# Values of the sink tokens by eight small transfers instead of selection matmuls, with a new order table

## The chip, the cores and the metric

The kernel runs on one core of one Trainium2 chip. A time is the device time in microseconds (us) of one execution. Before the change it is 243.45 us, the median of three runs (242.84, 243.45 and 244.1).

A core has five engines that each work through a list of instructions in order: PE (TensorE, matmuls; its weight loads are shown apart as PEld), DVE (VectorE), ACT (ScalarE), POOL (GpSimd) and SP (SyncE, which here only issues transfers). Matmuls write to PSUM, which has eight banks; everything else lies in SBUF. Transfers (DMAs) are issued by POOL, where an instruction of 0.7 to 1 us builds the descriptors, or by SP and ACT, and all of them are carried by the same 16 DMA engines.

## The reference

Two steps, in float32 at the reference and mostly bfloat16 in the kernel. First attention with a window of 128 keys and four "sink" keys (the first four of each sequence), for 4 batches, 8 heads, 768 positions and 64 values a head:

```python
scores = scale * np.matmul(q, k.transpose(0, 1, 3, 2))
keep = is_sink | in_window            # pos < 4, or 0 <= rel < 128
scores = np.where(keep, scores, -1e9)
a = np.exp(scores - max); a = a / (sum(a) + 1e-9)
x = np.matmul(a, v)                   # then (B*S, H*D) = (3072, 512)
```

Then a gated feed-forward layer on the 3072 rows:

```python
xn = x / np.sqrt(np.mean(x * x) + 1e-6) * rms_g
g = xn @ w_gate;  val = xn @ w_val    # 512 -> 1536
out = (g * sigmoid(g) * val) @ w_out  # 1536 -> 512
```

## The kernel before

**Tiling.** The 3072 rows are 24 blocks of 128 (g = 0 to 23; batch b = g // 6, place t = g % 6), and six groups G of four blocks for the feed-forward part. For each block the q, k and v tiles are loaded (POOL casts them to bfloat16 on the way; the first q and k come as float32 on SP's queue and are cast by DVE or ACT). q and k are turned to have the head's values on partitions: the first eight blocks by PE transposes with a copy (line 492, operations kp and qp), the others by a DMA transpose that SP issues (line 506). Then come scores (PE, lines 532, 548, 610), exp (ACT), masks (DVE, or POOL for late blocks), the product with v (av, lines 649 to 671), the division by the row sums (DVE; each v tile has a 65th column of ones that gives the sums), the root mean square and the scaling (xr, line 714), and the transposition of x (PE for the first eight blocks, line 729; a DMA transpose on SP from block 8 on, line 741). The feed-forward part follows: gate (g) and value (v) products, line 1000, tanh on ACT, two multiplications on DVE (lines 1013, 1023), the output product (o, line 1033), its copy to SBUF by ACT (line 1041) and a store of 256 KB issued by SP (line 1045).

**The sinks.** For the blocks with t of 2 and more the four sink keys lie outside the window. Their scores for all eight heads are made in one small product (ss, line 772), so that partition 32 x + 4 i + s (x = h // 2, i = h % 2) of the tile esk holds the exponential for head h and sink s. To multiply it with the values in one matmul (line 653), the tile vsk must hold, on partition 32 x + 4 i + s, the value row of sink s in the columns of head h and zero in the columns of the other heads. It is made in two halves for each batch: a matmul with the constant sel (line 754) copies the first four rows of v to all partitions, and DVE multiplies the result from PSUM with the head mask headm (line 763), two matmuls and two multiplications per batch, eight of each in all.

**The order.** The program is written as a list of some 1058 operations, numbered as they are declared. Each has a cost, what it needs and what it gives. The order on each engine is a table written out by hand (ORDER, lines 146 to 205), one list of numbers an engine. The class Plan (lines 35 to 143) goes through the table with its costs and its model of the transfers (land, line 59), to merge the five lists into one order of emission and to give each PSUM product a bank. Waits between engines follow from the data: an engine does not pass an instruction whose operands are not there, even where later ones could run. The parts that matter here:

- POOL's list begins with two selects for the constants ident and bias (lines 338, 344), then the loads: q and k of block 1, v of block 0, blocks 2 and 3 and the gate and value weights interleaved, then q of block 4, v of block 3, and so on. Only so many POOL loads are outstanding at a time; the next issue waits for a landing.
- PE's list begins with small matmuls on a zero tile (warm, line 468) among the first real work.
- SP's list has k and q of block 0 and the row of the scaling weights, then nothing until the DMA transposes of block 8 (near 47 us in the profile), with x transposes and stores from then on.
- DVE's list begins with the memsets.

## Time and profile before

| | before |
|---|---|
| median of three runs | 243.45 us |
| the profiled execution | 242.75 us |
| its span, first to last instruction | 241.0 us |
| PE busy | 235.0 us (98%) |
| DVE busy | 187.0 us (78%) |
| ACT busy | 122.3 us |
| POOL busy | 89.9 us |
| read from and written to HBM | 28.31 and 6.29 MB |
| matmuls of line 754 (vs) | 8, of 128 x 260 |
| multiplications of line 763 (vsk) | 8, 0.42 us each |

The profile is one execution. Its page lists the busy time of each engine, then the span in 40 slices (a digit is a busy share in tenths; PEclk is the TensorE clock that was granted, as a share of full speed), the DMA queues, and the chain of work that ended last. Other views cut out a stretch of time, list the instructions of an engine in order, or collect the instructions that touch one tile. Matmuls are pipelined: the duration of one in the profile includes its drain, which overlaps the next one, so the start of the next tells what it took of PE's time. A load's landing is the moment its semaphore is complete. A number in the text that isn't in a quoted line is a start, an end or a landing from the same trace.

### The profile page before, as it was taken

What the parts mean: (1) busy time and instruction counts of PE and PEld (TensorE: products, weight loads), DVE (VectorE), ACT (ScalarE), POOL (GpSimd) and SP (SyncE); (2) the same over time, 40 slices, a digit from 0 to 9 for tenths busy, and PEclk for the clock granted to TensorE, in tenths of its full rate; (3) what the DMA queues carried; (4) which work ended last, traced back from release to release, by engine and by line L of the source; (5) the groups of instructions that cost most, each with busy time, mean ns of one, the idle gap of its engine ahead of it and who ended that gap; (6) DMA issues with size and microseconds to landing.
All of it is one profiled execution on the core that took longest, in us unless ns stands there. A gap on an engine that the chain in (4) does not pass through costs nothing.

```text
span 241.0 us, 5846 instructions
## 1 busy us (share of the span) xinstructions
PE 235.0 (98%) x2324; PEld 149.8 (62%) x2324; DVE 187.0 (78%) x482; ACT 122.3 (51%) x267; POOL 89.9 (37%) x116
## 2 busy tenths in 40 slices
PE   6999999999999999999999999999999999999994
PEld 3469987875788676786886544445545444444443
DVE  2489979998999999999998999974599965436430
ACT  3775577477867565346754373461762222304211
POOL 8976885587555475200062123045340000000000
PEclk9679999999999999999999999999999999999999
DMA  9999999999999999999997809510241130103014
GB/s 125 148 183 188 184 184 187 164 136 150 141 137 149 180 165 146 159 180 169 141 153 70 109 0 112 115 40 0 87 47 22 21 112 0 69 18 131 3 50 167
DMA packets 113581, 27.38 MB, mean 114 GB/s; under 512 B 103697, under 2 KB 110609, under 8 KB 113554
## 3 DMA queue, kind: packets, MB, share of 16 engines
q0 software_dynamic: 81760, 13.90, 77.5%
q1 hardware_dynamic: 31650, 12.99, 29.8%
q8 instruction: 18, 0.29, 0.5%
q10 hardware_dynamic: 144, 0.13, 0.2%
q14 instruction: 9, 0.07, 0.1%
HBM read 28.31 MB, written 6.29 MB: 144 GB/s over the span
## 4 chain that ended last, share of the span: by engine, by line
PE 85%; DMA 7%; POOL 5%; issue 0%; DVE 0%; POOLq 0%
PE o L1033 25%; PE v L1000 24%; PE g L1000 23%; DMA wv<-in_moe_w_val_dram 4%; DMA q<-in_q_dram 3%; PE s L610 3%; PE av L668 2%; PE av L663 2%; PE av L653 2%; POOL wg L446 1%; POOL q L400 1%; POOL v L404 1%; PE o_last L1051 1%; POOL k L400 1%; PE s L532 1%; POOL wv L446 1%
## 5 line engine op out<-in xcount | busy, mean ns | idle before, releaser
L1000 PE MATMUL v<-xnt,wv 128*128 128x128 bf16 (+2 forms) x528 | 73.3, 282 | 0.0
L1000 PE MATMUL g<-xnt,wg 128*128 128x128 bf16 (+2 forms) x528 | 70.9, 282 | 0.0
L1033 PE MATMUL o<-wo,hT 128*128 128x512 bf16 x276 | 67.7, 379 | 0.0
L1007 ACT ACTIVATE th<-g 128x512 bf16<-128x512 f32 x72 | 41.6, 600 | 45.0 <-PE g L1000 40.0
L1013 DVE SCALAR_TENSOR_TENSOR p<-th,g 128x512 bf16<-128x512 bf16 x72 | 47.5, 682 | 17.6 <-ACT th L1007 17.4
L1000 PEld LDWEIGHTS <-wg 128*128 128x128 bf16 x528 | 43.2, 98 | 19.6 <-DMA wg<-in_moe_w_gate_dram 0.2
L1023 DVE TENSOR_TENSOR hT<-p,v 128x512 bf16<-128x512 bf16 x72 | 47.8, 682 | 9.6 <-PE v L1000 8.9
L1000 PEld LDWEIGHTS <-wv 128*128 128x128 bf16 x528 | 42.7, 98 | 19.9 <-issue 0.7
L1033 PEld LDWEIGHTS <-hT 128*128 128x128 bf16 x276 | 25.7, 98 | 26.0 <-issue 0.4
L644 POOL TENSOR_SCALAR_AFFINE_SELECT e<-e 128x512 bf16<-128x512 bf16 x20 | 12.6, 652 | 51.1 <-ACT e L619 50.8
L619 ACT ACTIVATE e<-s 128x384 bf16<-128x384 f32 x52 | 22.8, 498 | 15.4 <-PE s L610 15.3
L404 POOL DMA_DIRECT2D v<-in_v_dram x24 | 21.4, 890 | 9.1 <-DMA q<-in_q_dram 5.7
L690 ACT ACTIVATE sq<-x 128x512 bf16<-128x512 bf16 x24 | 15.3, 636 | 17.9 <-DVE x L682 17.7
L400 POOL DMA_DIRECT2D k<-in_k_dram x23 | 20.4, 888 | 8.5 <-DMA wo<-in_moe_w_out_dram 2.7
L400 POOL DMA_DIRECT2D q<-in_q_dram x23 | 20.5, 890 | 7.7 <-DMA k<-in_k_dram 4.5
L1041 ACT ACTIVATE osb<-o 128x512 f32<-128x512 f32 x23 | 13.5, 602 | 19.0 <-PE o L1033 19.0
L682 DVE TENSOR_TENSOR x<-av,rden 128x256 bf16<-128x256 f32 x48 | 20.4, 425 | 1.7
L714 DVE SCALAR_TENSOR_TENSOR xr<-x,r,gb 128x512 bf16<-128x512 bf16 x24 | 18.0, 752 | 0.8
L668 PE MATMUL av<-v,e 128*128 128x65 bf16 x192 | 17.8, 196 | 0.2
L583 ACT ACTIVATE e<-s 128x512 bf16<-128x512 f32 (+1 forms) x36 | 16.0, 528 | 2.8 <-PE s L532 2.3
L663 PE MATMUL av<-v,e 128*128 128x65 bf16 x160 | 15.5, 193 | 0.0
L668 PEld LDWEIGHTS <-e 128*128 128x128 bf16 x192 | 13.4, 99 | 2.6 <-DVE e L594 0.4
(78 smaller groups left out, 199.8 us busy)
## 6 DMA issues: line engine op xcount, KB each, us to landing
out_dram<-osb SPq DMA_DIRECT2D x23, 256.0 KB, 2.3
v<-in_v_dram POOLq DMA_DIRECT2D x24, 128.0 KB, 9.7
q<-in_q_dram POOLq DMA_DIRECT2D x23, 128.0 KB, 10.0
k<-in_k_dram POOLq DMA_DIRECT2D x23, 128.0 KB, 9.5
wo<-in_moe_w_out_dram POOLq DMA_DIRECT2D x2, 768.0 KB, 11.0
wg<-in_moe_w_gate_dram POOLq DMA_DIRECT2D x5, 256.0 KB, 8.2
wv<-in_moe_w_val_dram POOLq DMA_DIRECT2D x5, 256.0 KB, 8.6
stage<-in_k_dram SPq DMA_DIRECT2D x1, 256.0 KB, 3.2
```

Source lines behind the costliest of these rows:

```text
L400: nc.gpsimd.dma_start(out=T[name, g], in_=block_of(src, g))
L404: nc.gpsimd.dma_start(out=V16[b][:, t, :, 0:D], in_=block_of(v, g))
L619: nc.scalar.activation(out=e_tile(g)[:, x:x + 2, 0:TW], in_=BANK.pop(("s", g, u, hi))[:, 0:2 * TW].rearrange("p (j c) -> p j c", c=TW), fu ...
L663: nc.tensor.matmul(out=dest, lhsT=T["e", g - 1][:, x, P:2 * P], rhs=V16[b][:, t - 1, h, :], start=(t == 1), stop=False, skip_group_check=True,
L668: nc.tensor.matmul(out=dest, lhsT=T["e", g][:, x, 0:P], rhs=V16[b][:, t, h, :], start=(t == 0), stop=True, skip_group_check=True,)
L682: nc.vector.tensor_tensor(out=T["x16", g][:, 4 * u:4 * u + 4, :], in0=pvv[:, :, 0:D], in1=rden.unsqueeze(2).to_broadcast((P, 4, D)), op=AL ...
L714: nc.vector.scalar_tensor_tensor(out=T["xr", g], in0=T.pop(("x16", g)).rearrange("p h d -> p (h d)"), scalar=r[:, 3:4], in1=gb, op0=ALU.mu ...
L1000: nc.tensor.matmul(out=ps[:, i * n:(i + 1) * n], lhsT=w_sb[:, kt, ft * P:(ft + 1) * P], rhs=T["xnt", G][:, kt, cols], start=(kt == 0), sto ...
L1007: nc.scalar.activation(out=T["th", key], in_=BANK[("g", key)], func=ACT.Tanh, scale=0.5,)
L1013: nc.vector.scalar_tensor_tensor(out=T["p1", key], in0=T.pop(("th", key)), scalar=1.0, in1=BANK.pop(("g", key)), op0=ALU.add, op1=ALU.mult,)
L1023: nc.vector.tensor_tensor(out=T[hk][:, i:i + n, cols], in0=T.pop(("p1", key)).rearrange("p (n c) -> p n c", n=n), in1=BANK.pop(("v", key)) ...
L1033: nc.tensor.matmul(out=BANK[("o", G, tb)], lhsT=T["h", G, ft // 4][:, ft % 4, tb * P:(tb + 1) * P], rhs=wo[:, ft, :], start=(ft == 0), sto ...
```

## The change

The matmuls with sel, the tile sel and the copy that made it go. A tile vsink (128 x 4 batches x 65, float32) is set to ones by a DVE memset; eight transfers on SP's queue, one a head, put the four sink rows of v of all batches on partitions 32 x + 4 i to 32 x + 4 i + 3 (each 4 partitions x 4 batches x 64 values). For each batch one DVE multiplication of 128 x 520 makes vsk from vsink and headm. The 65th column stays one, as in the v tiles.

The planner's transfer model is changed: POOL loads are counted less late (a factor of 1.15 for 1.4 early on; 450 ns instead of 1000 ns added after 9 us), SP's transposes and stores 300 ns later. All five lists of the table are new. Since the numbers shift by nine behind the constants, the lists are told here by name:

- POOL: the first load (q of block 1) comes ahead of the two selects, bias then ident; k,2 and q,2 change places, as do some of the weight loads: the last four gate blocks now come in the order 10-11, 8, 9, ahead of all of value 8 to 11, whose order is 9, 10-11, 8. q of block 4 follows the same loads as before.
- DVE: the memset of vsink is first, then bias, ident, zeros; the constant masks come before the casts, and both first casts (k and q of block 0) are DVE's. The product vsk of batch 0 stands behind the scaling of block 0 by its sums and ahead of its xr; that of batch 1 stands among the multiplications of group 0.
- SP: after the row of scaling weights the eight small transfers (heads 6, 1, 4, 5, 3, 2, 7, 0). The DMA transposes begin q8, q9, k8, q10, k9, q11, k10, k11, then the store of block 3, q12, k12, the store of block 0, q13, q14, k14, the store of block 1, k13, k15, x8, q15, x9. Before, it was q8, k8, q9, k9, q10, q11, k10, k12, k11, q13, q12, the store of block 1, k13, q14, the store of block 0, q16, x8, x9.
- PE: k of block 1 is turned before the first scores. The list from the first gate product up to the turning of q of block 4 has the same members. Later, units move by up to some us; the scores of blocks 11 and 12 and the gate products of group 2 come earlier among the rest.

The core of the diff, and SP's list:

```diff
-            r["POOL"] = begin + (1.4 * work if begin < 8500 else work)
+            r["POOL"] = begin + (1.15 * work if begin < 8500 else work)
...
-            return r["POOL"] + 520 + (1000 if r["POOL"] > 9000 else 0)
+            return r["POOL"] + 520 + (450 if r["POOL"] > 9000 else 0)
...
-        return r["TR"] + (550 if ring == "TR" else 850) + min(late, 5000)
+        return r["TR"] + (850 if ring == "TR" else 1150) + min(late, 5000)
...
     "SP": """
-14 16 18 312 313 327 328 342 357 343 372 358 393 371 646 394 408 641 438 326 341 423 651
+23 25 27 21 16 19 20 18 17 22 15 315 330 316 345 331 360 346 361 653 374 375 638 393 408
...
-    sel = const.tile([P, P], BF16, name="sel")
+    vsink = const.tile([P, B, VW], FP32, name="vsink")
...
-    def make_sel():
-        nc.vector.tensor_copy(
-            out=sel.rearrange("p (a s) -> p a s", s=NS),
-            in_=ident[:, 0:NS].unsqueeze(1).to_broadcast((P, P // NS, NS)),
-        )
+    def make_headm():
...
+    dve(260, lambda: nc.vector.memset(vsink, 1.0), gives=["vsink1"], prio=-95)
+
+    def load_sink(h):
+        r = h // 2 * SW + h % 2 * NS
+        nc.sync.dma_start(
+            out=vsink[r:r + NS, :, 0:D], in_=v[:, h, 0:NS, :].rearrange("b s d -> s b d"),
+        )
+
+    for h in range(H):
+        sp(430, 2600, lambda h=h: load_sink(h), ["vsink1", "grow"], [("vsink", h)], -70 + h)
...
-    def sink_v(b, half):
-        nc.tensor.matmul(
-            out=bank(("vs", b, half))[:, 0:HW], lhsT=sel,
-            rhs=V16[b][:, 0, 4 * half:4 * half + 4, :], start=True, stop=True,
-        )
...
+    def sink_v(b):
+        T["vsk", b] = sink.tile([P, H, VW], BF16, name="vsk")
         nc.vector.tensor_tensor(
-            out=T["vsk", b][:, hs, :],
-            in0=BANK.pop(("vs", b, half))[:, 0:HW].rearrange("p (h c) -> p h c", c=VW),
-            in1=headm[:, hs].unsqueeze(2).to_broadcast((P, 4, VW)), op=ALU.mult,
+            out=T["vsk", b], in0=vsink[:, b:b + 1, :].to_broadcast((P, H, VW)),
+            in1=headm.unsqueeze(2).to_broadcast((P, H, VW)), op=ALU.mult,
         )
```

## The prediction

> **What bounds the kernel now.** I read the page first, for the busiest engine and the granted clock, then the windows by stage.
>
> ```profile
> span 241.0 us, 5846 instructions
> ...
> PE 235.0 (98%) x2324; PEld 149.8 (62%) x2324; DVE 187.0 (78%) x482; ACT 122.3 (51%) x267; POOL 89.9 (37%) x116
> ...
> PEclk9679999999999999999999999999999999999999
> DMA  9999999999999999999997809510241130103014
> ```
>
> ```profile
> 6.00:12.00 6.00, 5.80 (x46) 2.97 (x44) 2.99 (x15) 4.71 (x13) 6.00 (x9) 0.68 2.06 148
> 12.00:18.00 6.00, 5.76 (x78) 3.99 (x76) 4.82 (x20) 4.50 (x14) 4.51 (x6) 0.75 1.55 183
> ...
> 24.00:30.00 6.00, 6.00 (x108) 5.84 (x106) 5.50 (x10) 3.27 (x7) 5.14 (x6) 1.00 1.70 185
> ...
> 100.00:120.00 20.00, 20.00 (x241) 15.31 (x239) 18.73 (x51) 12.14 (x27) 0.00 (x0) 1.00 1.50 159
> ```
>
> The second fence gives a stretch, its length, the busy time of PE, PEld, DVE, ACT and POOL, the granted clock, the DMA share and GB/s. From 24 us on PE is never idle at full clock. A busy PE can still be slow, so I compared start-to-start times with widths: after 21 us the sum of all lost time is under 1 us. So behind 21 us PE's own work is the time; only less PE work, or a new wait, changes it.
>
> Next the chain of waits up to 32 us, and PE in order of time around its last line:
>
> ```profile
> 14.14 9.69 DMA wv<-in_moe_w_val_dram
> 23.84 0.30 issue
> 24.13 7.73 DMA q<-in_q_dram
> 31.86 0.05 issue
> 31.91 0.23 PE q L492
> ```
>
> ```profile
> 26.94 3.90 PE L1000 MATMUL g<-xnt,wg 128*128 128x128 bf16 x64
> 30.68 1.13 PE L1000 MATMUL v<-xnt,wv 128*128 128x128 bf16 x16
> 31.91 0.40 PE L492 MATMUL q<-ident,q 128*128 128x128 bf16 x4
> ```
>
> The transposition of q of block 4 waits for a load that lands at 31.86, 0.26 us after PE is ready; that load could be issued only when an older one had landed. So whatever PE gains before 32 us it hands back there: this landing starts the long saturated stretch. PE's work list ahead of that transposition has the same members in both tables (but for the two selection matmuls of batch 0), so the new table can't fill the wait.
>
> **The matmuls that go.** The rows of the tile vs, and one of its matmuls in order of time with its follower:
>
> ```profile
> L754 PE MATMUL vs<-v,sel x8: 274/274/398, 9.0 to 136.8; 128*128 128x260 bf16 x8
> L763 DVE TENSOR_TENSOR vsk<-vs,headm x8: 419/421/429, 9.5 to 138.1; 128x260 bf16<-128x260 f32 x8
> ```
>
> ```profile
> 57.62 0.27 PE L754 MATMUL vs<-v,sel 128*128 128x260 bf16 x1
> 57.73 0.81 PE L1033 MATMUL o<-wo,hT 128*128 128x512 bf16 x3
> ```
>
> The 274 ns include the overlapped drain; the slot is 57.73 - 57.62 = 0.11 us. Two of the eight lie before 14 us, where their 0.2 and 0.3 us vanish in the wait for q; six lie in the saturated stretch: five of 0.111 and one of 0.122, **-0.68 us**, all on the path.
>
> **DVE.** Per batch two multiplications of 0.42 us become one of 520 columns. The nearest row below is 128x512 at 0.68 (line 1023), the end above 0.84; I take 0.69, so 0.6 us less in all. The copy into sel (0.27) goes; the memset of vsink is added, from the memsets of 64 and 128 words (0.11, 0.17) about 0.30. DVE is 94% busy from 40 to 140 us, but PE doesn't wait for it; its cover is the PE stream. Nothing for the end. The product of batch 1 moves to about 28.6 us, where DVE has 0.23, 0.55 and 0.32 us idle before 33.5, enough for its 0.69. The memset stands first on DVE and delays the memsets of bias, ident and zeros by up to 0.5 us: the warm-up matmuls start at about 1.6 instead of 1.06, in time for the k block that lands at 4.05.
>
> **SP, start.** Eight issues at 0.45 to 0.57 us (the three issues now there) keep SP until about 6.2 us; its next instruction now comes at 47 us, so nothing queues behind them. They move 8 x 4 KB = 32 KB. Their price is in the DMA, which is full. The nearest transfers are the stage loads:
>
> ```profile
> stage<-in_k_dram SPq DMA_DIRECT2D x1, 256.0 KB, 3.2
> stage<-in_q_dram SPq DMA_DIRECT2D x1, 256.0 KB, 3.9
> ```
>
> Issued at 0.81 and 1.32, they land 1.2 us apart, so 256 KB cost 1.2 us and 32 KB cost 0.15, if spread like those. At worst they all lie on a quarter of the engines and hold each later load 0.6. The Trainium skill (DMA: Bandwidth & Descriptors, "Why a DMA increments its semaphore by 16 and not by 1") speaks for the worst: the engine count follows the slowest dimension, so a four-partition transfer uses four engines, the lowest-numbered. By that rule the sum would be 0.45 us higher than by the row; the trace names no engine, so it does not decide.
>
> **POOL, start.** The first load is issued ahead of the two selects: at about 0.8 (when SP starts) instead of 1.76, the later ones 0.35 earlier (0.8 + 1.01 + 0.29 + 0.25 + hops, against 2.77). But from 8 us on the loads wait on transfers, not issue (issue to landing grows from 4.5 to 9.7 us). Gain 0 to 0.35, and the first load now competes with the q stage load: its cast may be 0.5 to 0.9 late, repaid by the shorter PE list up to 18 us. Landing of q,4: -0.2 to +0.6; I take **-0.1** (0.25 gained, 0.15 paid, after the row of the same kind).
>
> **The new order behind 32 us.** I laid PE's new list out from q,4, each unit with its start-to-start time of before, and set it against landings. SP's list is what matters, since it waits in order:
>
> ```profile
> 71.44 2.64 SPq L506 DMA_TRANSPOSE qkT<-q  x2
> 74.18 0.57 SPq L1045 DMA_DIRECT2D out_dram<-osb  x1
> ```
>
> ```profile
> DMA to landing us min/median/max: 2.4/7.9/9.3
> ```
>
> The first is SP in order of time, where its first store goes out; the second is of the q and k transposes (line 506). The new list issues two stores and one more transpose before 71 us. The scores of block 12 move from 84.2 to 80.6; they need a transpose that was issued at 71.44 and landed at 80.13: 0.5 us to spare instead of 3. The first gate matmul of group 2 moves from 98.35 to 96.8 and needs the transpose of x of block 9. SP gives it out after k,15 has landed (82.89) and three transposes of 1.24: 86.6, plus 7.9 is 94.5. Three more transfers of 0.9 to 1.2 us ahead push it to 97.2 to 98.1. So the new wait is 0 (its 2.3 us to spare hold) to 1.3; with the longest latency, 9.3, it is 2.7. Latencies now don't grow with more transposes under way (8.1 us for one issued with one other under way, 8.1 with five), so I stay near the low end: **+0.4**. Lateness of several places doesn't add up, because each pushes all behind it.
>
> Sum: -0.68 - 0.1 + 0.4 = -0.38 on a span of 241.0. The profiled execution took 242.75 us in all, 0.70 below the median of 243.45 (242.84 to 244.1); I put the change on the median: **243.1 us**. About 0.5%, 1.2 us, is what this kernel's measurement can tell from no change.
>
> **Rivals.**
> 1. *Late transposes (the other side).* The moved stores hold the loads and SP's list back, and PE stands before block 12 or group 2. For: DMA at 9 tenths until slice 21, PE 98% busy, so no cover. Against: PE hardly waits today with the same latencies. Price 2.0 to 2.7, net +1.2 to +1.9: 244.7 to 245.4. It decides from 2.0 us of waiting on (0.78 gained, 1.2 to the bound). Chance 0.28.
> 2. *Small transfers on four engines.* q,4 at +0.45 beside my value: 243.5. Chance 0.14.
> 3. *A wait in place of the matmul.* The product of batch 0 stands on DVE ahead of the first block's scaling and waits for all eight transfers. The last issue is at about 5.7; with 3.9 us, as the stage load, it lands at 9.6, before the 10.9 at which DVE comes to it. With 7.9, as the transposes, 13.6: scaling 2 us late, then 2.3 us to spare on PE, no loss. Only past 14.5 does it cost: 0.5 to 1: 243.8. Chance 0.05.
> 4. *No new wait, loads 0.35 early.* -0.68 - 0.2: 242.6, and 242.3 if the 0.26 us at q,4 and the 0.15 us that PE waits at 28.7 go too. Chance 0.18.
> 5. *The clock.* It is 0.68 and 0.75 in 6:18, granted half from 8.2 to 15.0. One more half-rate stretch as long as half of that (3.4 us) costs up to 1.7, less 0.7 us of idle PE up to 32: +1.0, 244.1. The Trainium skill (TensorE: Matmul & The Clock Gate, "What's actually happening") says that the gate judges activity in free-running windows of about 3.4 us, so moving PE's work by half a microsecond may lose or win a whole window; the trace agrees in length, 6.8 us being two. Chance 0.05.
>
> The forecast has 0.30. The bound of faster is 242.2, and the runs of before spread by 0.6 us to each side: half of rival 4 and a fifth of the forecast fall below it, 0.15. Slower (244.7) is rival 1 and 0.05 of rivals 2, 3 and 5, 0.33; the rest, 0.52, is within 0.5%. Range: from the low draws of rival 4 (242.2) into rival 1 (245.2). The likeliest alone: 242.6 to 243.6.
>
> **What would show it.** No vs row, eight more SP issues near 2.4 to 6.2 us; the wait at q,4 still there within 0.5 us of 31.86; PE busy 20.00 in each 20 us behind it. Wrong if PE shows idle time before block 12's or group 2's matmuls over 1 us, if q,4 lands past 32.5, or if the end is 1.2 us earlier, which nothing here pays for.

## The result, and the profile after

The changed kernel takes 244.85 us (median; 244.42 to 245.46), against 243.45 (242.83 to 244.1) for the kernel before beside it: a ratio of 1.0056, 95% interval 1.0039 to 1.0073. It is slower by 1.4 us, where 0.35 us less was forecast.

The page of the changed kernel: its span, the busy time by engine, then the granted clock and the DMA share in 40 slices.

```profile
span 242.7 us, 5866 instructions
...
PE 232.4 (96%) x2316; PEld 148.9 (61%) x2316; DVE 187.8 (77%) x481; ACT 119.9 (49%) x264; POOL 90.0 (37%) x116
...
PEclk9999999999999999999999999999999999999999
DMA  9999999999999999999630999321300332001204
```

Less PE work and a longer span: 2.6 us less busy, 1.7 us more span. The clock was full from 8.4 us on in this execution, where the profiled one of before had it at half from 8.2 to 15.0. (The row PEclk has no record of the first microseconds and shows them as full. PE's matmuls of 128 columns start 0.107 us apart up to 8.4 us and 0.056 us behind that, so PE ran at half rate there; in the kernel before it did so up to 4.7 us, and again from 8.2 to 15.0.) That is where part of the 2.6 us comes from, and it bought nothing: the first gate matmul starts 0.97 us earlier (16.87 for 17.84), and the turn of q of block 4 (q,4 from here on; a turn is the transposition of a q or k block) starts at 32.13 for 31.91.

The windows of the changed kernel, columns as in the prediction (stretch, length, busy time of PE, PEld, DVE, ACT, POOL, clock, DMA share, GB/s):

```profile
12.00:18.00 6.00, 4.30 (x79) 3.40 (x77) 4.67 (x21) 5.04 (x16) 4.63 (x7) 1.00 1.65 180
...
24.00:30.00 6.00, 5.82 (x105) 5.64 (x103) 5.13 (x11) 2.77 (x5) 4.95 (x7) 1.00 1.66 186
...
36.00:44.00 8.00, 7.33 (x118) 5.12 (x116) 6.96 (x19) 4.92 (x12) 4.36 (x5) 1.00 1.70 187
80.00:86.00 6.00, 5.50 (x67) 4.16 (x65) 5.59 (x22) 1.91 (x6) 4.52 (x7) 1.00 2.11 155
...
100.00:120.00 20.00, 20.00 (x242) 15.09 (x240) 18.74 (x51) 11.44 (x28) 0.87 (x1) 1.00 1.48 156
135.00:142.00 7.00, 6.41 (x54) 3.43 (x51) 6.22 (x22) 3.23 (x8) 4.37 (x5) 1.00 1.65 148
```

PE is full between 100 and 120 as before, and has holes in 36:44, 80:86 and 135:142. The view of PE's waits from 22 to 145 us names them (line, what it waited for, us in total, times, longest); for the kernel before the same view has no line at all:

```profile
PE k L498 <- DMA k<-in_k_dram: 0.7, 1, 0.7
PE g L993 <- DMA xnt<-xr: 0.6, 1, 0.6
PE s L538 <- DMA qkT<-q: 0.5, 1, 0.5
PE g L993 <- DMA wg<-in_moe_w_gate_dram: 0.4, 1, 0.4
PE v L993 <- DMA wv<-in_moe_w_val_dram: 0.2, 1, 0.2
```

And where they stand, PE in order of time (start, length, what, idle time before it):

```profile
32.13 0.40 PE L498 MATMUL q<-ident,q 128*128 128x128 bf16 x4
...
41.14 0.40 PE L498 MATMUL k<-ident,k 128*128 128x128 bf16 x4 [0.67 <-DMA k<-in_k_dram]
...
82.35 0.61 PE L538 MATMUL s<-qkT 64*128 64x256 bf16 x8 [0.51 <-DMA qkT<-q]
...
139.52 1.69 PE L993 MATMUL g<-xnt,wg 128*128 128x512 bf16 x7 [0.59 <-DMA xnt<-xr]
```

Three waits behind the turn of q,4: the turn of k of block 5, the scores of block 12, the first gate of group 3. From here on a wait is counted from start to start: the time from the start of the matmul before, less what that matmul takes of PE when nothing is late. That gives 0.834, 0.669 and 0.755 us, more than the idle times shown, which leave out the drain of the matmul before. (The idle time at k of block 5 is put down to its load, which landed at 41.09.) The sum is 2.26 us.

**The balance closes.** From the start of q,4's turn to the start of the last output matmuls (o_last) the trace gives 234.93 - 31.91 = 203.02 us before and 236.58 - 32.13 = 204.45 after. Take the waits away: 203.02 - 0.12 = 202.90 before (0.12 in all, near 43 us), 204.45 - 2.26 = 202.19 after. The difference, 0.71, is the 0.68 of the six matmuls. So the matmuls' time was gained, and waits that weren't there before took it and 1.4 us more.

**Why these transfers are late.** SP's queue in order of time, the changed kernel from 63 us:

```profile
63.38 3.23 SPq L512 DMA_TRANSPOSE qkT<-k  x2
66.71 0.54 SPq L1038 DMA_DIRECT2D out_dram<-osb  x1
67.43 1.25 SPq L512 DMA_TRANSPOSE qkT<-q  x1
68.77 1.28 SPq L512 DMA_TRANSPOSE qkT<-k  x1
70.11 0.57 SPq L1038 DMA_DIRECT2D out_dram<-osb  x1
74.55 6.83 SPq L512 DMA_TRANSPOSE qkT<-q  x2
```

SP had its two stores out at 66.7 and 70.1 and stood free at 70.7. It waited for the load of q of block 13, whose turn went out at 74.55, where before it went out at 71.44. That load was issued at 59.74 (59.46 before) and landed at 74.53 (71.42 before); k of block 13, issued at 60.60, at 77.03 (72.38). The queues of both kernels between 60 and 72 us, from the issue of this load on (packets, MB, time of the packets as a share of 16 engines' span), before:

```profile
q0 software_dynamic: 8423, 1.06, 144.9%
q1 hardware_dynamic: 2370, 0.57, 51.7%
```

and after:

```profile
q0 software_dynamic: 6406, 0.81, 112.5%
q1 hardware_dynamic: 3547, 0.86, 73.8%
```

q0 carries POOL's loads, q1 what SP issues; in this stretch that is turns alone, since the data of the two stores moves behind 72 us. The sum is nearly the same (1.63 and 1.67 MB), but the turns have 0.29 MB more and the loads 0.25 MB less. The new list sends its turns up to those of block 12 closer together, and what they move arrives while q and k of block 13 wait for theirs. (Between 70 and 78 us, the stretch that an expectation below speaks of, SP's queue moved 0.92 MB for 0.41. There the excess is the data of the two stores, 256 packets of 2 KB, and the turns' part is as before, 0.40 for 0.41 MB.) Sharing need not be all of it. Between the issue and the landing of q of block 13 the DMA engines stood nearly idle, at 3 tenths or under in slices of 0.2 us, for 1.8 us in three gaps (1.0 us in two gaps before); no run here shows what makes these gaps.

The gate of group 3 is another place: on SP the x of block 14, which was ready at 121.39, stands behind the x of block 15, which DVE finished at 133.06. It went out at 134.32 and PE waited for it until 139.52.

**The start.** POOL in order of time:

```profile
1.32 1.01 POOL L406 DMA_DIRECT2D q<-in_q_dram  x1 [0.80 <-POOLq L1137]
2.42 0.30 POOL L344 TENSOR_SCALAR_AFFINE_SELECT bias<-bias 128x128 bf16<-128x128 bf16 x1
2.67 0.29 POOL L338 TENSOR_SCALAR_AFFINE_SELECT ident<-ident 128x128 bf16<-128x128 bf16 x1
2.90 0.91 POOL L406 DMA_DIRECT2D k<-in_k_dram  x1
4.14 1.09 POOL L410 DMA_DIRECT2D v<-in_v_dram  x1 [0.32 <-DVE masks L361]
```

The first load is 0.44 earlier (1.76 before), the third is 0.51 later (3.63 before): v of block 0 needs the 65th column of ones, a DVE memset; in the new list it stands behind the cut of ident, and ident is now made on POOL behind a load (the row names the DVE instruction next to that memset). The gate weights 4-5 land at 22.04 (20.04 before), behind 6-7, and PE stands 0.571 and 0.350 us at 21 and 25 us for weights. All of this lies ahead of q,4.

The added parts themselves:

```profile
L383 SPq DMA_DIRECT2D vsink<-in_v_dram x8: 275/300/302, 2.7 to 5.1; - x8
L761 DVE TENSOR_TENSOR vsk<-vsink,headm x4: 690/694/701, 11.5 to 146.7; 128x520 bf16<-128x520 f32 x4
L379 DVE MEMSET vsink<- x1: 275/275/275, 0.9 to 0.9; 128x260 f32 x1
```

### The profile page after: what moved, and what is told of

It is laid out like the page before. It is cut to its first block, busy times and chain, and to the rows that moved or that the text cites. A ratio compares the mean times of both kernels' runs of the same rounds, so it can differ in the third digit from the quotient of the medians.

```text
span 242.7 us, 5866 instructions
## 1 busy us (share of the span) xinstructions
PE 232.4 (96%) x2316; PEld 148.9 (61%) x2316; DVE 187.8 (77%) x481; ACT 119.9 (49%) x264; POOL 90.0 (37%) x116
## 4 chain that ended last, share of the span: by engine, by line
PE 59%; DMA 24%; POOL 10%; DVE 4%; issue 2%; POOLq 0%; SPq 0%
PE v L993 18%; PE g L993 18%; PE o L1026 16%; DMA wg<-in_moe_w_gate_dram 7%; DMA q<-in_q_dram 6%; DMA wo<-in_moe_w_out_dram 5%; POOL v L410 4%; DMA qkT<-q 3%; POOL q L406 3%; POOL k L406 2%; DMA xnt<-xr 2%; PE s L616 2%; PE o_last L1044 1%; DVE hT L1016 1%; PE av L674 1%
## 5 line engine op out<-in xcount | busy, mean ns | idle before, releaser
L993 PE MATMUL g<-xnt,wg 128*128 128x128 bf16 (+2 forms) x528 | 71.7, 282 | 1.1 <-DMA xnt<-xr 0.6
L993 PE MATMUL v<-xnt,wv 128*128 128x128 bf16 (+2 forms) x528 | 71.7, 282 | 0.3 <-DMA wv<-in_moe_w_val_dram 0.2
L650 POOL TENSOR_SCALAR_AFFINE_SELECT e<-e 128x512 bf16<-128x512 bf16 x20 | 13.1, 676 | 43.1 <-ACT e L625 42.9
L625 ACT ACTIVATE e<-s 128x384 bf16<-128x384 f32 x52 | 22.3, 501 | 11.9 <-PE s L616 11.9
L696 ACT ACTIVATE sq<-x 128x512 bf16<-128x512 bf16 x24 | 15.3, 639 | 16.4 <-DVE x L688 16.3
L674 PE MATMUL av<-v,e 128*128 128x65 bf16 x192 | 16.5, 193 | 1.8 <-ACT qkT L505 1.6
L674 PEld LDWEIGHTS <-e 128*128 128x128 bf16 x192 | 12.7, 97 | 3.4 <-ACT e L589 1.3
L669 PE MATMUL av<-v,e 128*128 128x65 bf16 x160 | 14.7, 193 | 0.0
## 6 DMA issues: line engine op xcount, KB each, us to landing
wo<-in_moe_w_out_dram POOLq DMA_DIRECT2D x2, 768.0 KB, 11.9
```

The lines of the kernel that those rows point to most:

```text
L625: nc.scalar.activation(out=e_tile(g)[:, x:x + 2, 0:TW], in_=BANK.pop(("s", g, u, hi))[:, 0:2 * TW].rearrange("p (j c) -> p j c", c=TW), fu ...
L674: nc.tensor.matmul(out=dest, lhsT=T["e", g][:, x, 0:P], rhs=V16[b][:, t, h, :], start=(t == 0), stop=True, skip_group_check=True,)
L993: nc.tensor.matmul(out=ps[:, i * n:(i + 1) * n], lhsT=w_sb[:, kt, ft * P:(ft + 1) * P], rhs=T["xnt", G][:, kt, cols], start=(kt == 0), sto ...
```

## The experiments

Two theories stand against each other. *The order*: the new table makes the waits, the transfers are harmless. *The transfers*: the eight small transfers hold back the loads (rival 2), and the waits follow from that. The expectations speak of theory O and theory T. Ratios are to the kernel before, run beside each experiment; brackets hold 95% intervals. In diffs of the table the numbers are operations; what they are is said beside it.

### The two halves alone

*a_old_order* keeps the transfers, the memset and the one product a batch, with the planner's constants and all five lists of before; the transfers stand on SP behind the row of scaling weights, where the change has them.

```diff
-            r["POOL"] = begin + (1.15 * work if begin < 8500 else work)
+            r["POOL"] = begin + (1.4 * work if begin < 8500 else work)
...
-            return r["POOL"] + 520 + (450 if r["POOL"] > 9000 else 0)
+            return r["POOL"] + 520 + (1000 if r["POOL"] > 9000 else 0)
...
-        return r["TR"] + (850 if ring == "TR" else 1150) + min(late, 5000)
+        return r["TR"] + (550 if ring == "TR" else 850) + min(late, 5000)
...
```

> The eight transfers with the order of before (the selection matmuls taken out of PE's list, one product in place of two on DVE, the memset of vsink behind the other first memsets, the eight transfers behind the row of scaling weights on SP, and the planner's old constants). Theory O (the new order makes the waits): the transfers cost nothing and 0.68 us of PE goes, so 0.3 to 1.0 us faster than before, 242.4 to 243.1; the wait at q of block 4 stays near 31.9 and the first output weights land near 38.1. Theory T (the transfers hold the loads back, 1.2 us from the first output weights on): q of block 5's k lands near 41.1 as in the changed kernel, where the old order has 1.1 us to spare, and the time is 243.2 to 244.2, no faster than before.

Measured: 243.1 us, 0.9995 [0.9973, 1.0017].

*b_new_order* is the other half: the kernel before, with its matmuls, sel and two products a batch, and the new constants and lists. The vs matmuls of a batch stand behind the v product of the batch's first block; the diff is the one above turned round, and the lists.

> The new order and the planner's new constants with the selection matmuls of before, put behind the products with v of the first block of each batch (their two products on DVE behind its scaling). Theory O: the waits of the changed kernel stay (0.8 us before k of block 5 is turned, 0.7 at block 12, 0.75 at group 3) and 0.7 us of matmuls come back, so 245 to 246. Theory T: without the transfers the loads land as before, the wait at k of block 5 goes, and the time is 243.5 to 244.5.

Measured: 246.53 us, 1.0133 [1.0108, 1.0157].

So the order alone costs 1.3%, more than the whole change and more than theory O had for it (245 to 246). The transfers with the old order leave the time as it was. That does not show that they cost nothing: the 0.68 us of the matmuls alone would make a ratio of 0.997, the lower end of a's interval, and theory O's sign, q,4 landing near 31.9, failed (32.62 in a); theory T's, k of block 5 near 41.1, failed too (40.60). In b, q,4's turn comes at 32.92 and from there to the last matmuls it takes 205.24 us, 2.2 more than before; in a it takes 202.65, 0.37 less, with a wait of 0.29 for an x transpose at 98.64. The place of the vs matmuls in b was my choice, so its last tenths are not the order's alone.

### The transfers taken out of the changed kernel

*c_no_transfers* is the changed kernel less the eight transfers; it leaves out the values of the sink tokens.

```diff
     def load_sink(h):
         r = h // 2 * SW + h % 2 * NS
-        nc.sync.dma_start(
-            out=vsink[r:r + NS, :, 0:D], in_=v[:, h, 0:NS, :].rearrange("b s d -> s b d"),
-        )
```

> The changed kernel without the eight transfers: vsink keeps the ones of its memset, so the values of the sink tokens are left out; all else is as in the changed kernel. Theory O: within 0.3 us of the changed kernel, 244.5 to 245.1, and k of block 5 still lands near 41. Theory T: k of block 5 lands near 39.9 to 40.2 and 0.8 to 1.2 us go, 243.6 to 244.1.

Measured: 245.09 us, 1.0084 [1.0052, 1.0116]; q,4 landed at 33.04 and k of block 5 at 41.31, so theory T's sign (39.9 to 40.2) did not come. Without the transfers the kernel is no faster, and the load that starts the long stretch came later than with them. The waits stood elsewhere: 0.66 us for a value weight at 25.8 and 1.54 us for the x transposes of group 3 at 138.4; none at block 5, none at block 12.

### Single waits

*f_stores_later* puts the two stores (653, 638) behind the turn of q of block 13 (393):

```diff
-23 25 27 21 16 19 20 18 17 22 15 315 330 316 345 331 360 346 361 653 374 375 638 393 408
+23 25 27 21 16 19 20 18 17 22 15 315 330 316 345 331 360 346 361 374 375 393 638 653 408
```

> The changed kernel with two stores of SP's list (blocks 0 and 3) moved from ahead of the transposes of block 12 and 13 to behind that of q of block 13. If these two stores push the loads from q of block 13 on: it lands near 71.5 to 73 instead of 74.5, the 0.67 us of PE before the scores of block 12 go, and the time falls by 0.5 to 0.7 us unless a later wait takes them. Rival: the loads are late for another reason, q of block 13 still lands after 74 and the time stays within 0.2 us of the changed kernel.

Measured: 244.4 us, 1.0044 [1.0029, 1.0059]. The load of q of block 13 landed at 75.05, no earlier: the stores don't hold it. The wait at block 12 was 0.32 us, that at group 3 0.30, and one of 0.49 came at group 2 (98.36).

*g_x14* puts the x transpose of block 14 (422) ahead of that of block 15 (437):

```diff
-389 798 506 470 437 422 507 803 542 525 455 813 560 484 561 524 468 505 543 808 541 523
+389 798 506 470 422 437 507 803 542 525 455 813 560 484 561 524 468 505 543 808 541 523
```

> The changed kernel with one swap in SP's list: the transpose of x of block 14, ready at 121.4, ahead of that of block 15, which waits for DVE until 133.1. Theory L (this last wait holds the end, and the earlier ones were absorbed by it): the wait of 0.75 us (1.5 without the transfers) before group 3 goes, the time falls by 0.6 to 0.9, to 243.9 to 244.3. Rival (each wait adds to the end for itself, and x of block 15 is late anyway, because of the five loads that POOL issues from 134 on): less than 0.3 us, 244.6 or more.

Measured: 244.45 us, 1.0052 [1.0025, 1.0078]. The time lies between the two ranges of the expectation. The wait at group 3 is gone; 0.26 us at 71 (for DVE), 0.42 us at the scores of block 13 and 0.46 at group 2 stand in the profile instead.

*e_k5_back* moves the turn of k of block 5 (257) one output product (639) later:

```diff
-584 599 585 237 600 222 605 614 610 229 255 231 239 615 241 174 634 257 639 644 235 259
+584 599 585 237 600 222 605 614 610 229 255 231 239 615 241 174 634 639 257 644 235 259
```

> The changed kernel with one entry of PE's order moved: the turn of k of block 5 one unit (one output matmul group of 0.86 us) later, where it waits for the load of that k; in the changed kernel's profile it waited 0.834 us at 40.09. Strong form of theory O: the 0.834 us is gained, ratio to the kernel before 1.0020 to 1.0030. Absorption: the wait at 40 us falls to near nothing, but PE then reaches the transposes that went out on SP at 66 to 85 us, and the first gate of group 3 at 139.5 us (where the changed kernel waited 0.755 us for an x transpose that was issued behind an x which DVE finished at 133.06), so much earlier, and waits there for it: the waits at 82 us and 139 us together are longer by over half of it, and the ratio is 1.004 to 1.006.

Measured: 244.66 us, 1.0057 [1.0037, 1.0076]. The wait at 40 us is gone and the time is that of the changed kernel: absorbed. The waits behind it in this profile: 0.29 at 51, 0.20 at 65, 0.21 at 74, 1.05 at block 12, 0.17 at 93, 0.66 at group 2, 0.58 at group 3.

So the wait at block 5 is not worth its length: 0.83 us off would be a ratio of 1.0022, below the interval. What PE gained there it lost at the next late transfers. For the wait at group 3 (g_x14) 0.75 us off would be 1.0025, at the very end of the interval; f_stores_later only halved the wait that it aimed at. These two point the same way and don't show it.

### The changed kernel and the kernel before once more

> The kernel before once more, for a second profile: how far the landings of one and the same program move. If q of block 4 lands within 0.2 us of 31.86, the 32.6 seen with the old order and the eight transfers is the transfers' doing (theory T: four engines hold each load back); if it lands near 32.6 too, it is the spread between executions, and the transfers cost at most 0.2 us.

> The changed kernel once more, unchanged, with a second profile: which of its waits belong to the order and which to the one execution. Theory O: the ratio is 1.004 to 1.007 again, and the waits over 0.3 us stand at the same instructions: a gate or value matmul behind a late weight load at 21 to 26 us, the scores of block 12 at 81 to 82 us, and the first gate of group 3 at 138 to 140 us. If the loss of the changed kernel were an accident of its one profiled execution, the waits would stand elsewhere, and the ratio could be anything from 1.000 to 1.006. For the turn of k of block 5 at 40 us (0.834 us in the first profile) I expect a wait whose length follows the landings: with q,4 at 32.1 or earlier 0.8 us, with q,4 at 32.6 near nothing, since the load of that k came at 40.5 to 40.6 where q,4 came late.

The kernel before: 242.96 us, span 241.2, q,4 landed at 32.02. By the first expectation that speaks for theory T, but it sets one execution against one, and the next two kernels don't bear it out: with the transfers q,4 landed at 31.90 (k_old_start), without early ones at 32.74 (i_hybrid). There is no wait over 0.12 us behind 22 us, and again 203.02 us from q,4's turn to the last matmuls. The changed kernel: 245.2 us, 1.0071 [1.0044, 1.0099]; q,4's turn at 32.40, and no wait at block 5, whose k landed at 40.33 (41.09 in the first profile). Instead: 1.07 at 64.9 (scores), 0.28 at block 12, 0.75 at group 2, 0.71 at group 3; these four sum to 2.81 us. The long stretch took 205.08 us. Block 12 had less than the 0.3 us expected of it, and block 5 none, with q,4 between the two cases of the expectation. The same loss in two executions, by waits that in part stand at other places.

### The start

*k_old_start* is g_x14 with POOL's first 25 entries and DVE's first memsets in their old order (first the select of ident, 8, and of bias, 9; on DVE zeros, 7, first and the memset of vsink, 14, seventh). Shown are the heads of the two lists, DVE's first:

```diff
-14 1 0 7 11 10 2 12 24 26 150 6 148 179 13 165 163 200 171 167 192 194 169 170 196 208
+7 0 1 2 11 10 14 12 24 26 150 6 148 179 13 165 163 200 171 167 192 194 169 170 196 208
...
-29 9 8 30 31 36 35 38 32 34 33 41 42 37 45 43 39 46 44 51 47 49 50 52 48 53 40 57 54 56
+8 9 29 30 31 35 36 38 34 32 33 41 42 37 43 45 39 44 46 49 48 51 47 52 50 53 40 57 54 56
```

> The swap of x of block 14 and, on top, the start of before: POOL's two selects and its first 23 loads in the old order, DVE's first memsets in the old order with that of vsink behind them. Theory O: v of block 0 is no longer issued late (3.6 instead of 4.1), the gate weights 4 to 7 land 0.7 earlier, q of block 4 0.3 to 0.5 earlier, and the time is 0.3 to 0.6 below the swap alone, 243.4 to 243.9. Rival: q of block 4 lands when all loads ahead of it have, in whatever order, so nothing comes of it, within 0.2 us of the swap alone.

Measured: 243.92 us, 1.0019 [0.9996, 1.0041]. q,4 landed at 31.90 and k of block 5 at 39.87, as in the kernel before (31.86, 39.85), with the eight transfers in place. PE came to q,4's turn only at 32.30, in an execution in which its matmuls ran at half rate up to 16.7 us (0.107 us apart for 128 columns, then 0.056). No wait was left at weights or at block 5. Two were left, in order of time:

```profile
91.69 0.54 PE L619 MATMUL s<-qkT 64*64 64x192 bf16 x24 [0.29 <-DMA qkT<-k]
...
98.06 0.70 PE L996 MATMUL g<-xnt,wg 128*128 128x256 bf16 x5 [0.27 <-DMA xnt<-xr]
```

From start to start 0.457 and 0.439 us, both for transposes that stand on SP behind others which are not ready.

### The transfers late instead of early

*i_hybrid* has the old order; batch 0's values come by the two matmuls, and the transfers for the other batches go out behind the turn of k of block 8 on SP, near 51 us.

```diff
-            out=vsink[r:r + NS, :, 0:D], in_=v[:, h, 0:NS, :].rearrange("b s d -> s b d"),
+            out=vsink[r:r + NS, 1:B, 0:D],
+            in_=v[1:B, h, 0:NS, :].rearrange("b s d -> s b d"),
...
+    def sink_first(half):
+        nc.tensor.matmul(
+            out=bank(("vs", 0, half))[:, 0:HW], lhsT=sel,
+            rhs=V16[0][:, 0, 4 * half:4 * half + 4, :], start=True, stop=True,
+        )
...
```

> The old order and the planner's old constants; batch 0 keeps its selection matmuls, which stand where PE waits anyway, and the eight transfers bring only batches 1 to 3 and are issued behind the transpose of k of block 8, near 51 us, where SP waits for a load. Theory T: without early transfers q of block 4 lands as before, and the whole 0.68 us show: 242.6 to 242.9, 0.3 us or more below the old order with early transfers (0.9995 of before). Theory O (the early transfers cost nothing): the same as the old order with early transfers, 243.0 to 243.4. A new wait before the first sink product of batch 1, near 68 to 70 us, would show that 51 us is too late.

Measured: 244.11 us, 1.0031 [1.0015, 1.0047]. SP in order of time:

```profile
50.43 1.25 SPq L521 DMA_TRANSPOSE qkT<-k  x1
51.72 6.36 SPq L391 DMA_DIRECT2D vsink<-in_v_dram  x8
58.34 1.19 SPq L521 DMA_TRANSPOSE qkT<-q  x1
```

and PE:

```profile
66.87 0.29 PE L794 MATMUL ss<-qkT,ksk 128*32 128x256 bf16 x4 [1.41 <-DMA qkT<-q]
```

That is outside both ranges; the third case of the expectation came, the late first sink product. The eight issues took 2.69 us at the start of the program (4 KB each) and 6.36 us here (3 KB each). The last two went out at 55.86 and 57.83, each some 2 us behind the one before it. The turn of q of block 9 went out at 58.34, where before it went out at 54.53, and PE waited 1.58 us for it. q,4 landed at 32.74 with no early transfer at all.

### SP's list mended

*m_sp_order* is k_old_start with two more moves on SP: the turn of k of block 13 (394) right behind that of q of block 13 (393), and the turn of q of block 15 (423) behind the x of block 9 (344).

```diff
-... 361 653 374 375 638 393 408
-409 643 394 424 329 423 344 438 718
+... 361 653 374 375 638 393 394
+408 409 643 424 329 344 423 438 718
```

> This is the kernel with POOL's and DVE's old start and xt,14 ahead of xt,15, with two more moves on SP and nothing else: the k transpose of block 13 comes right behind the q transpose of block 13 (it was issued at 82.92, its source having landed at 75.57), and the q transpose of block 15 comes behind the x transpose of block 9 instead of ahead of it (the x was ready at 86.45, the transpose went out at 90.14). Theory O, in its strong form (the order's loss is the sum of its waits, and each that goes is gained): the two waits that were left in that kernel's profile, 0.457 us at 91.12 for the scores of block 13 and 0.439 us at 97.4 for the first gate of group 2, both fall under 0.1 us, and nothing follows in their place. Span 241.7 - 0.9 = 240.8; time 0.3% under the kernel before, ratio 0.996 to 0.999. Rival, absorption (a wait that goes lets PE come earlier to the next transfer, which is not earlier): the two go, but more than half of the 0.9 us is back in waits behind 97 us, the x transposes of blocks 10 and 11 or those of group 3 above all; span 241.3 or more, ratio 1.000 to 1.003. Rival, transfers (the eight small transfers hold something that no wait shows): the same ratio, but with the waits gone and PE's busy time longer.

Measured: 243.13 us, 0.9982 [0.9969, 0.9995]. The two waits are gone. The profiled execution was a late one (243.67 us, q,4 landed at 32.66) and had new waits of 0.26 us at 71 (for DVE) and 0.56 us at the scores of block 12; its span was 241.9, not 240.8.

> The kernel with the old start of POOL and DVE and the three moves on SP once more, unchanged, with a second profile, on the same chip as the changed kernel. Its first profile (span 241.9) fell in an execution whose load of q of block 4 landed at 32.66, where other executions with the same start had 31.86 to 31.90, and its time there (243.67) was above its median (243.13). Strong form of theory O: ratio 0.996 to 0.9995 again, and in an execution with q,4 landed by 32.0 the span is 241.0 or less. If the wait at 81.67 us (0.556, the scores of block 12) stands there again at the same length, the two moves on SP have only pushed the wait forward, the span is 241.4 to 241.9 whenever q,4 lands, and the ratio is 0.9985 to 1.001. Against the changed kernel the ratio is 0.991 to 0.994 by the first, 0.993 to 0.996 by the second.

Measured: 243.16 us, 0.9991 [0.9973, 1.0009], span 241.4, q,4 landed at 32.12. The scores of block 12 waited 0.83 us at 80.93, for the turn of q of block 13, whose load landed at 74.07. So by the wait and the span it is the second branch, part of the 0.9 us had only moved forward; the ratio lies in the ranges of both. Against the changed kernel, which ran beside it at 245.2, it is faster by 0.8%; from the kernel before it can't be told apart.

### What holds the load of q of block 13

*q_turns_later* puts the turns of q and k of block 12 (374, 375) behind that of q of block 13:

```diff
-... 361 653 374 375 638 393 394
+... 361 653 638 393 374 375 394
```

> A probe of what holds the load of q of block 13, not a version to keep: in the kernel of m_sp_order the two turns of block 12 (q and k, some 0.13 MB each) are put behind the turn of q of block 13 on SP. In the trace of the kernel before, SP's queue moved 0.42 MB between 70 and 78 us and POOL's loads 0.71 MB; in the changed kernel it was 0.92 MB and 0.37 MB, with the sum the same. If it is the turns in flight that hold the loads, q of block 13 lands 1 to 3 us earlier than in m_sp_order and m_again (74.8, 74.1), so at 71.5 to 73.3. PE then waits at the scores of block 12 for the turns of its own block instead, which go out at 73 to 75 and land some 7 us later: 1 to 3 us of wait at 81 us, and a longer time (1 to 2 us). If the load is held by something else (its own queue, its issue), it lands at 74 to 75.

*p_q13_first* changes POOL's list instead: v of block 12 (81) goes out behind q and k of block 13 (82, 83).

```diff
-... 79 80 81 82 83 84 ...
+... 79 80 82 83 81 84 ...
```

> The kernel of m_sp_order with one load moved on POOL: v of block 12 goes out behind q and k of block 13 instead of ahead of them. In m_again the q of block 13 landed at 74.07, 7.4 us behind the q of block 12 (66.64), its turn went out at once, and the scores of block 12 waited 0.828 us for it at 80.93. The v of block 12 has 2.2 us of landing to itself (67.4 to 69.6). If the wait at 81 us is what keeps that kernel from the sum of its waits: q of block 13 lands 1 to 2 us earlier (72 to 73), the wait falls under 0.2 us, the span falls to 240.6 to 240.9 in an execution with q,4 at 32.1, and the ratio is 0.995 to 0.998. If it is absorbed again: the wait falls, but others behind it (scores of block 13 at 91, the first gate of group 2 at 97, that of group 3 at 139) take over half of it, and the ratio is 0.998 to 1.000. If the landing of q of block 13 is not a matter of the loads ahead of it on its own queue, it lands at 74 to 75 as before and nothing changes.

In q_turns_later, one execution, the load landed at 72.29 (74.78 in m_sp_order, 74.07 in m_again), 1.8 to 2.5 us earlier. It had been issued 0.6 to 0.8 us earlier too (58.56 for 59.15 and 59.35); from issue to landing it took 13.7 us for 15.6 and 14.7. So the turns in flight do hold it, by 1 to 2 us. As expected, PE then waited for the turns of block 12, and it took 245.01 us:

```profile
83.71 0.61 PE L541 MATMUL s<-qkT 64*128 64x256 bf16 x8 [2.36 <-DMA qkT<-k]
```

In p_q13_first it was issued at 58.40 and landed at 70.66, 12.3 us, so the loads ahead of it on its own queue hold it as well. Over all profiles it landed at 70.69 to 72.67 with the old lists (four) and at 73.37 to 75.18 with the new list on SP (ten, without the two kernels of this section). PE's windows of that kernel, columns as above:

```profile
36.00:44.00 8.00, 8.00 (x133) 5.97 (x131) 7.43 (x20) 5.61 (x14) 4.04 (x5) 1.00 1.71 186
80.00:86.00 6.00, 6.00 (x71) 4.53 (x69) 5.63 (x21) 2.48 (x7) 3.19 (x5) 1.00 2.25 131
...
135.00:142.00 7.00, 7.00 (x77) 3.72 (x76) 6.46 (x22) 3.29 (x9) 4.07 (x5) 1.00 1.76 153
```

The holes are closed: behind q,4 one wait of 0.26 us is left, at 71.4, for DVE. From q,4's turn to the last matmuls it takes 202.67 us, 0.35 less than before. The time is 243.25 us, 0.9989 [0.997, 1.0007], all the same, since q,4 landed at 32.62 in the profiled execution and its turn started at 32.84, 0.93 later than before. The waits went as in the first case of the expectation, and the time is that of the second. In this execution more was lost ahead of the stretch than was won in it.

### All in one table

"Long stretch" is from the start of q,4's turn to that of the last output matmuls.

| kernel | time, us | ratio | q,4's turn | long stretch |
|---|---|---|---|---|
| before, two profiles | 243.45 | 1 | 31.91, 32.07 | 203.02, 203.02 |
| after, two profiles | 244.85, 245.2 | 1.0056, 1.0071 | 32.13, 32.40 | 204.45, 205.08 |
| a_old_order | 243.1 | 0.9995 | 32.67 | 202.65 |
| b_new_order | 246.53 | 1.0133 | 32.92 | 205.24 |
| c_no_transfers | 245.09 | 1.0084 | 33.09 | 203.95 |
| f_stores_later | 244.4 | 1.0044 | 33.40 | 203.44 |
| g_x14 | 244.45 | 1.0052 | 32.60 | 203.46 |
| e_k5_back | 244.66 | 1.0057 | 32.64 | 205.13 |
| k_old_start | 243.92 | 1.0019 | 32.30 | 203.21 |
| i_hybrid | 244.11 | 1.0031 | 32.78 | 204.08 |
| m_sp_order, two profiles | 243.13, 243.16 | 0.9982, 0.9991 | 32.71, 32.17 | 203.09, 203.16 |
| p_q13_first | 243.25 | 0.9989 | 32.84 | 202.67 |
| q_turns_later | 245.01 | | 32.11 | 205.05 |

## Why the prediction was wrong

The forecast was 243.1, no change that can be told; what came is rival 1, the late transposes, in the time that it was given (244.7 to 245.4) and near its price (2.0 to 2.7 us of waiting; 2.26 and 2.81 measured). That its price fits is in part luck. It put the lateness down to the moved stores, and without them ahead (f_stores_later) the load of q of block 13 was as late; and in the first profile only one of the three waits, block 12, stands where it said. Of the prediction's own signs of being wrong none came in that profile (0.67 us at block 12, q,4 landed at 32.09), while its sign of being right, PE busy 20.00 in each 20 us, failed (19.33, 19.50 and 19.41 in three of the stretches).

On the span the forecast was -0.68 - 0.1 + 0.4 = -0.38. The traces have -0.71 for the matmuls, +0.22 for q,4's turn and 2.26 - 0.12 = +2.14 for the waits, +1.65 in all.

**The matmuls that go, -0.68: right.** Long stretch less its waits: 202.90 before, 202.19 after, 202.36 in a_old_order, 202.41 in p_q13_first: 0.5 to 0.7 us.

**DVE: right.** The product takes 0.69 us, the memset 0.28, and no wait for vsk stands on PE's path of the changed kernel. Rival 3 didn't come: the product of batch 0 started at 11.51, behind other DVE work, and waited for nothing.

**SP's start, rival 2: no price seen, and the figures off.** The eight issues took 0.30 each and were over at 5.4, not 0.45 to 0.57 and 6.2. Behind a first update at its issue, each transfer raised its semaphore four times more. The Trainium skill (DMA: Bandwidth & Descriptors, "Why a DMA increments its semaphore by 16 and not by 1") has a transfer of four partitions on four engines, and the trace agrees with the count. The price that I had worked out from it, 0.45 us on the loads, isn't seen: q,4 landed at 31.90 to 33.35 in eleven profiles with the early transfers and at 31.86 to 33.04 in five without. Within such a spread a smaller price could not be seen.

**POOL's start, -0.1: not borne out, probably wrong in sign.** I took the first load to be issued at 0.8 and the later ones 0.35 us earlier. The first went out at 1.32, 0.44 earlier, and v of block 0 0.51 later, since I hadn't followed DVE's list to the memset that it waits for. With the new start q,4's turn came at 32.13 to 33.40 in seven profiles, with the old one at 31.91 to 32.84 in nine, so the two overlap. Putting the old start back moved the ratio from 1.0052 to 1.0019, though the intervals overlap; in the two profiles 0.30 us of it is q,4's turn.

**"Whatever PE gains before 32 us it hands back": right.** The first gate matmul came 0.97 us earlier, and it was lost at weights and at q,4. In the changed kernel's second profile, at half rate up to 16.7 us, it came at 18.33, 1.46 us later than in the first, and q,4's turn was only 0.27 later. The clock (rival 5) fell well for the changed kernel in its first profile and gave nothing. The Trainium skill (TensorE: Matmul & The Clock Gate, "What's actually happening") has windows of about 3.4 us; the profiles agree in that the half-rate stretches of the clock's record were 3.4 and 6.8 us long, and that full rate began at other times in other executions of one kernel (8.4 and 16.7 us in the changed one).

**"The new wait is 0 ... to 1.3", taken at +0.4: this is the step that failed.** Each wait by itself is within its bounds (0.67 and 0.28 at block 12, 0 and 0.75 at group 2; the x of block 9 landed at 97.7, within the 97.2 to 98.1 forecast), but the waits behind 32 us came to 2.26 and 2.81. Three things were wrong in it:

- I set the new list against the landings of before. That the scores of block 12 had 0.5 us to spare rested on a turn that landed at 80.13; its source landed 3.1 us later. "Latencies now don't grow" is true of the turns (issued at 74.55, landed at 82.22, 7.7 us) and not of the loads: q of block 13 took 14.8 us from issue to landing for 12.0, k of block 13 16.4 for 11.9. Turns and loads share the DMA (0.86 and 0.81 MB between 60 and 72 us, 0.57 and 1.06 before), and a list that sends the turns closer together takes the time from the loads, whose data the next turns wait for.
- I looked at two places, block 12 and group 2. Two others were in the diff: the turn of k of block 5, moved 0.86 us earlier with 1.09 to spare against the old landing (it came 1.24 later in the first profile, 0.48 later and without a wait in the second), and the x of block 14 put behind the x of block 15 on SP.
- "Lateness of several places doesn't add up" is half true. Within one execution it did add up, since each later transfer was later still (0.83 + 0.67 + 0.76). What holds is the other direction: the wait at block 5, taken away, wasn't gained (e_k5_back 1.0057 against 1.0056; g_x14 with 1.0052 and f_stores_later with 1.0044 point the same way).

**What stays open.** Where a_old_order, m_sp_order and p_q13_first lose what they gain in the long stretch: in the profiles it is the start, with q,4's turn at 32.2 to 32.8 for 31.9 to 32.1. Whether the memset of vsink, the transfers, the clock or only the draw of executions puts it there was not told apart. With the old start q,4 landed at 31.86, 32.02 and 32.74 (i_hybrid, with the memset) without early transfers, and at 31.90 to 32.66 in six profiles with them, which speaks against the transfers; the two profiles of m_sp_order, 32.71 and 32.17, show that executions of one kernel differ by as much. In k_old_start and p_q13_first PE itself came 0.40 and 0.22 us behind the landing, at half rate up to 16.7 and 16.8 us.

## What to carry to other kernels

A margin read from one trace ("this operand lands 0.5 us before it is needed") holds for the order that made the trace. When the new order itself moves transfers, ask first which loads share the DMA with them, and let every operand with less than a microsecond to spare count as late. In a chain of many such margins, count all the transposes and loads that move, not the two tightest, and don't price a wait that you remove at its length: look for the next late transfer first.

## What was not expected of the hardware

- DMA transposes take the time from loads that are already issued. With 0.86 MB of transposes between 60 and 72 us instead of 0.57, POOL's loads fell from 1.06 to 0.81 MB, and the load in question landed 3.1 us later; two turns out of the way made it 1 to 2 us shorter from issue to landing.
- Eight issues of small transfers took SP 2.69 us at 2.75 us (4 KB each, three transfers issued ahead of them) and 6.36 us at 51.7 us (3 KB each), where turns and POOL's loads were in flight.
- The row PEclk reads as full where it has no record. In k_old_start it is at 9 tenths throughout, and PE's matmuls of 128 columns start 0.107 us apart up to 16.7 us and 0.056 us behind.
- The landing of one load, with nothing changed ahead of it, varies by half a microsecond from execution to execution (q,4 at 32.66 and 32.12 in one kernel), as much as the whole effect that was to be forecast.
